# Seven-product output in one more tile, even and odd output rows, padded sums: a fused sparse attention and bilinear FFN on one Trainium2 core

## The chip, the cores and the metric

The kernel runs on one core of a Trainium2 chip. The metric is the device time in microseconds (us) of one execution. The program is one launch, with all inputs and outputs in DRAM (HBM). The page and the answers quoted below come from one profiled execution on that core.

## The reference: what is computed

The inputs are q, k and v of shape (8, 8, 576, 64) in float32 (batch, heads, sequence, head width), and three weight matrices.

```
scores = (q @ k^T) / 8
heads 0..3: keep pairs with 0 <= i - j < 32            (local)
heads 4..7: keep pairs with j <= i and i % 32 == j % 32 (strided)
attn   = softmax(scores) @ v
x      = attn as (8*576 = 4608 tokens, 8*64 = 512)
out    = ((x @ w_a) * (x @ w_b)) @ w_out
```

`w_a` and `w_b` are 512 x 1536 and `w_out` is 1536 x 512. The output is 4608 x 512 in float32.

## The kernel before

**Tiles and slots.** The FFN runs over nine tiles of 512 tokens (t = 0 to 8). Each tile is 16 slots. Slots 0 to 11 of a tile are `ffn_ab`: for one block f of 128 hidden columns, PE makes a = x w_a and b = x w_b in two PSUM banks (L545), ACT copies a to SBUF (L562), and DVE multiplies it by b into the bf16 tile `pf` (L565 or L567). Slots 12 to 15 multiply `pf` by `w_out`, a quarter of the tile's output work each. The attention of the next batch is laid between the slots by hand (`STEPS`, `LATER`): S steps are scores (PE L356), ACT's exponential (L364) and DVE's mask (L374); V steps multiply by v (PE L410 or L454), take the inverse of the sums on ACT (L463, L464), and write `xT` on DVE (L468, L470; in batches 0 and 1 it is DVE L418 and L433).

**Order.** The order of each engine's queue is the order in which the Python code issues its instructions; there is no reordering scheduler. `do(i, fn, ...)` puts a call at the end of slot i, counted over all tiles (slot 16 t + s). A wait is set by the tile framework wherever an instruction touches memory that an earlier one of another engine wrote or still reads. In many slots POOL copies one element of the slot's result (`pace`, L880), so that POOL's loads behind it are not issued too early.

**The output in two ways.** `ffn_y` (L726) is the plain product: for each 128 tokens, twelve matmuls of 128x512 (L730), one ACT copy (L736) and one store from the SP queue (L738). `ffn_ys` (L714) is used in the tiles that `FAST_Y` lists. It takes pairs of f blocks (g = 0 to 5, e = 0 or 1), halves of the tokens (i = 0 or 1) and halves of the output columns as a 2 x 2 block product, and computes it with seven products in place of eight. It needs

- sums of weights, `wf` (five kinds n, two DVE instructions each, `fast_w`, L174);
- sums and differences of `pf`, `ps` (five kinds, made by DVE in `fast_s`: L578 for kind 0, L580 for kinds 1 and 2, L582 for kinds 3 and 4), in seven instructions per tile at slots 4, 6, 8, 10, 11, 11 and 12, which cover pairs 0 to 1, 2 to 3, 2 to 5 or 4 to 5 (`slice(z0, z1)`);
- `y_plan` (L610): the products in the order 3, 4, 1, 7, 5, 2, 6, each of 2 x 6 matmuls of 128x256 (L650). The stationary operand is a slice of `pf` (products 3 and 4) or of `ps` (the rest). q = 0 or 1 chooses which 128 of a half's 256 tokens. Product 1 reads kind 0, product 5 kind 1, product 2 kind 2, product 6 kind 3, product 7 kind 4.

After the products ACT copies (L622, L633, L635), DVE adds (L626, L629, L631, L639), and POOL subtracts (issued by L824's helper, two per tile). `store_half` writes one half i in two stores from SP (`y_store`, L603 to L605), one for each q.

**The last tile.** `y_tail` (L656) makes the same products with q as the outer loop, so that the first half of the rows is stored while the second is computed. For q = 0 each product has its own bank. For q = 1 products 3, 5 and 4, 2 use the two banks of a tile `o`, and products 1, 6 and 7 the two banks of a tile `st`. The last product is cut in two, the second part in a bank of its own.

**Memory shared.** `ps` has the same buffer as the early loads of batches 0 and 1 (`shared`). `wf` is made in slots 33 to 42, that is in tile 2.

Of the kernel before, what the change touches and what calls it, by code (L numbers as in the profile page):

```python
# [7 lines left out]
F32 = mybir.dt.float32  # L8
BF16 = mybir.dt.bfloat16
I16 = mybir.dt.int16  # L10
ALU = mybir.AluOpType
# [12 lines left out]
PW = 344  # L24
VW = 128
WCH = (0, 2, 5, 8, 10, 12)
FAST_Y = (3, 4, 5, 6, 7, 8)


@with_exitstack  # L30
def kernel(
# [10 lines left out]
    nc = tc.nc  # L42
# [7 lines left out]
    FD = d_ff // 128  # L50
    TTOK = 512
# [6 lines left out]
    nat = ctx.enter_context(tc.tile_pool(name="nat", bufs=1))  # L58
    sb = ctx.enter_context(tc.tile_pool(name="sb", bufs=3))
    fsb = ctx.enter_context(tc.tile_pool(name="ffn", bufs=2))  # L60
    pst = ctx.enter_context(tc.tile_pool(name="pst", bufs=1, space=bass.MemoryType.PSUM))
    dram = ctx.enter_context(tc.tile_pool(name="dram", bufs=2, space=bass.MemoryType.DRAM))

    psum4 = {}
# [98 lines left out]

    FG = FD // 2
    HT = TTOK // 2
    HN = d_model // 2
    wf = wp.tile([128, 5, FG, HN], BF16, name="wf")
    wov = wo_sb.rearrange("p (g e) (j n) -> p e j g n", e=2, j=2)
# [14 lines left out]
    shared = {}  # L183

    def load_qk(b, strided, heads=range(HL), names="kq"):
        for nm in names:
            src = {"k": k, "q": q}[nm]
            if b < FIRST_D:
                n, R, h0 = (NP, RS, HL) if strided else (96, RL, 0)
                w0 = {"k6": 0, "q6": 1536, "k8": 3072, "q8": 5120}[f"{nm}{R}"]  # L190
                if b not in shared:
                    shared[b] = nat.tile([128, 5 * FD * TTOK // 4], BF16, tag="shared", name="shared")
                t = nats[b, nm, strided] = shared[b][:n, w0:w0 + HL * R * D].rearrange("p (h r d) -> p h r d", r=R, d=D)
                hs = slice(heads[0], heads[-1] + 1)
                nc.gpsimd.dma_start(out=t[:, hs], in_=src[b, h0:h0 + HL].rearrange("h (p r) d -> p h r d", r=R)[:, hs])  # L195
            elif strided:

                t = nat_s[nm]
                n = 32 if b == FIRST_D else YS
                for h in heads:  # L200
                    nc.gpsimd.dma_start(
                        out=t[32 * h:32 * h + n],
                        in_=bass.AP(tensor=src.tensor, offset=(b * H + HL + h) * S * D,
                                    ap=[[RS * D, n], [YS * RS * D, 3], [1, RS * D]]))
            else:
                if 0 in heads:
                    nats[b, nm, strided] = nat.tile([128, NY, D], BF16, tag=f"{nm}l", name=f"{nm}l")
                t = nats[b, nm, strided]
                for h in heads:
                    nc.gpsimd.dma_start(out=t[32 * h:32 * h + 32],  # L210
                                        in_=src[b, h].rearrange("(i y) d -> y i d", y=32))
            nats[b, nm, strided] = t
# [127 lines left out]
    ps = {}  # L340
# [190 lines left out]
    def mm_bank(shape):  # L531
        nm = "tp" if used[0] % 4 == 3 and used[0] >= 0 else "mm"
        used[0] += 1
        return psum4[nm].tile(shape, F32, tag=nm, name="mm")
# [13 lines left out]
    def ffn_ab(t, f, mid, ab=None):  # L548
# [13 lines left out]
        nc.scalar.copy(a_sb, ab[0])  # L562
        if t in FAST_Y:
            halves = lambda x: x.rearrange("p (a i s) -> p a i s", i=2, s=16)
# [5 lines left out]
    pss = {}  # L570

    def fast_s(t, n, gs):
        if t not in pss:
            pss[t] = nat.tile([128, 5 * FD * TTOK // 4], BF16, tag="shared", name="ps").rearrange("p (g m) -> p g m", g=FG)
        s = pss[t][:, gs]
        x = pfs[t].rearrange("p (g e) (i m) -> p g e i m", e=2, i=2)[:, gs]
        if n == 0:
            nc.vector.tensor_tensor(s[:, :, 0:HT], x[:, :, 0, 0], x[:, :, 1, 1], op=ALU.add)  # L578
        elif n == 1:
            nc.vector.tensor_tensor(s[:, :, HT:3 * HT].rearrange("p g (i m) -> p g i m", i=2), x[:, :, 0], x[:, :, 1], op=ALU.add)  # L580
        else:
            nc.vector.tensor_tensor(s[:, :, 3 * HT:].rearrange("p g (e m) -> p g e m", e=2), x[:, :, :, 1], x[:, :, :, 0],  # L582
                                    op=ALU.subtract)

    yst = {}

    def products(t):
        pf, s = pfs[t], pss[t]
        full = lambda e, i: (lambda g, q: pf[:, 2 * g + e, HT * i + 128 * q:HT * i + 128 * (q + 1)])
        summed = lambda n: (lambda g, q: s[:, g, HT * n + 128 * q:HT * n + 128 * (q + 1)])  # L590
        wsum = lambda n: (lambda g: wf[:, n, g])
        wfull = lambda e, j: (lambda g: wov[:, e, j, g])
        return {"3": ("a", full(0, 0), wsum(0)), "4": ("b", full(1, 1), wsum(1)), "1": ("c", summed(0), wsum(2)),
                "2": ("b", summed(2), wfull(0, 0)), "5": ("a", summed(1), wfull(1, 1)), "6": ("c", summed(3), wsum(3)),
                "7": ("d", summed(4), wsum(4))}
# [5 lines left out]
        return slice(HN * j, HN * (j + 1))  # L601

    def y_store(eng, t, y, i, q, n=slice(0, d_model)):  # L603
        rows = out[TTOK * t:TTOK * (t + 1), n].rearrange("(q a i s) c -> a s i q c", q=2, i=2, s=16)
        eng.dma_start(out=rows[:, :, i, q], in_=y[i][:, q, n])  # L605

    def y_bufs():
# [2 lines left out]
    def y_plan(t):  # L610

        plan, bank, v = products(t), {}, {}
        y = []

        def store_half(i):
            for q in range(2):
                y_store(nc.sync, t, y, i, q)

        def post(k):
            if k == "3":  # L620
                v["a"] = v["w"] = f32t("ya")
                nc.scalar.copy(v["a"], bank["a"])  # L622
                y.extend(y_bufs())
                v["y"] = y
            elif k == "4":
                nc.vector.tensor_tensor(v["w"], bank["b"], v["a"], op=ALU.add)  # L626
            elif k == "1":
                v["e"] = f32t("ye")
                nc.vector.tensor_tensor(v["e"], bank["c"], v["w"], op=ALU.add)  # L629
            elif k == "7":  # L630
                nc.vector.tensor_tensor(v["e"], v["e"], bank["d"], op=ALU.subtract)  # L631
            elif k == "2":
                nc.scalar.copy(y[1][:, :, col(0)], bank["b"])  # L633
            elif k == "5":
                nc.scalar.copy(y[0][:, :, col(1)], bank["a"])  # L635
                do(16 * t + 15, nc.gpsimd.tensor_tensor, y[0][:, :, col(0)], v["e"], y[0][:, :, col(1)], ALU.subtract)
                do(16 * t + 18, store_half, 0)
            else:
                nc.vector.tensor_tensor(v["w"], bank["c"], v["w"], op=ALU.add)  # L639
                do(16 * t + 17, nc.gpsimd.tensor_tensor, y[1][:, :, col(1)], v["w"], y[1][:, :, col(0)], ALU.subtract)  # L640
                do(16 * t + 19, store_half, 1)

        for k in "3417526":
            b, lhs, rhs = plan[k]
            new = b not in bank
            if new:
                bank[b] = mm_bank([128, 2, HN])
            for q in range(2):
                for g in range(FG):
                    nc.tensor.matmul(bank[b][:, q], lhsT=lhs(g, q), rhs=rhs(g), start=new and q == 0 and g == 0,  # L650
                                     stop=g == FG - 1, skip_group_check=True)
                    if g == FG - 1 and q == 1:
                        post(k)
                    yield v

    def y_tail(t):  # L656

        plan, y = products(t), y_bufs()
        w, e = f32t("ya"), f32t("ye")
        v = {"a": w, "y": y}  # L660
        for q in range(2):
            if q == 0:
                bank = {x: mm_bank([128, HN]) for x in "abcd"}
            else:
                o = psum4["o"].tile([128, 2, 512], F32, tag="o", name="end")
                st = pst.tile([128, 2, 512], F32, tag="st", name="end")
                bank = {"a": o[:, 0, :HN], "b": o[:, 1, :HN], "c": st[:, 0, :HN], "d": st[:, 1, :HN]}
            c21, c12, c22 = y[1][:, q, col(0)], y[0][:, q, col(1)], y[1][:, q, col(1)]
            wq, eq = w[:, q], e[:, q]
            seen = set()  # L670
            for k in "3412567":
                b, lhs, rhs = plan[k]
# [69 lines left out]
    with tc.manual_schedule(engines={ENG.PE, ENG.SP, ENG.Pool, ENG.DVE, ENG.Activation}):  # L742
# [10 lines left out]
        for x, src in ((raw[0], k), (raw[1], q)):  # L753
            nc.sync.dma_start(out=x[:96].rearrange("p (h r d) -> p h r d", h=2, d=D),
                              in_=src[0, 0:2].rearrange("h (p r) d -> p h r d", r=RL))
# [67 lines left out]
        def do(i, fn, *args):  # L823
            at.setdefault(i, []).append(lambda: fn(*args))  # L824
# [7 lines left out]
        for b in range(FIRST_D, B):  # L832
# [7 lines left out]
            else:  # L840
# [5 lines left out]
            gs = {2: (13, 13, 14, 14, 15, 16, 17, 17, 18, 18), 3: (8, 9, 10, 11, 12, 13, 14, 15, 16, 17)}.get(b) or (  # L846
                3, 5, 7, 9, 12, 13, 14, 15, 16, 17)
# [10 lines left out]
        do(17, rezero, 1)  # L858
        do(18, fill_v, vl_buf[1])
        do(19, fill_v, vs_buf[1])  # L860
        for n in range(5):
            for z in range(2):
                do(33 + 2 * n + z, fast_w, n, slice(3 * z, 3 * z + 3))
        for g in range(FG):
            for n in range(3 if g < FG - 1 else 1):
                do(16 * (NT - 1) + 2 * g + 1, fast_s, NT - 1, n, slice(g, g + 1))
# [45 lines left out]
```

The softmax here doesn't subtract the row's maximum and nothing guards it: scores larger than these inputs give would overflow.

## Time and profile before

| what | value |
|---|---|
| median of three runs | 337.68 us (337.02 to 338.57) |
| the profiled execution | 336.98 us, of which the span 335.3 us |
| mean granted TensorE clock | 0.998 |
| PE busy | 326.2 us, 97% |
| DVE busy | 254.7 us, 76% |
| ACT busy | 202.8 us, 60% |
| POOL busy | 173.4 us, 52% |
| moved by DMA | 37.60 MB, mean 112 GB/s |

The span runs from the first instruction to the last; 1.7 us of the profiled execution lie outside it. Busy shares are means over the whole span: the sections about 40 slices and the answers for single windows tell where an engine is full. A time such as 158.01 is counted from the start of the span. In a timeline line the first number is the start, the second how long the group of x instructions lasted from its first start to its last end. Matmuls overlap: a matmul of 128x512 is listed with 379 ns, but six of them follow each other in 1.30 us, so each takes 0.216 us of PE; eighty-four of 128x256 take 9.17 us, 0.109 us each. "Idle before" is the time that an engine stood still ahead of an instruction, and the releaser is who ended it.

### The profile page before, as it was taken

What the parts mean: (1) busy time and instruction counts of PE and PEld (TensorE: products, weight loads), DVE (VectorE), ACT (ScalarE), POOL (GpSimd) and SP (SyncE); (2) the same over time, 40 slices, a digit from 0 to 9 for tenths busy, and PEclk for the clock granted to TensorE, in tenths of its full rate; (3) what the DMA queues carried; (4) which work ended last, traced back from release to release, by engine and by line L of the source; (5) the groups of instructions that cost most, each with busy time, mean ns of one, the idle gap of its engine ahead of it and who ended that gap; (6) DMA issues with size and microseconds to landing.
All of it is one profiled execution on the core that took longest, in us unless ns stands there. A gap on an engine that the chain in (4) does not pass through costs nothing.

```text
span 335.3 us, 7662 instructions
## 1 busy us (share of the span) xinstructions
PE 326.2 (97%) x2814; PEld 201.8 (60%) x2814; DVE 254.7 (76%) x489; ACT 202.8 (60%) x329; POOL 173.4 (52%) x295
## 2 busy tenths in 40 slices
PE   8999999999999999999999999999999999999992
PEld 6654555455555555556999885568556844674472
DVE  5867566768878985799999999999877845738641
ACT  5663955468678865776587757875788533223320
POOL 8945836499956644765577457754312031312011
PEclk9999999999999999999999999999999999999999
DMA  9999999599999599969888998899123021003013
GB/s 155 148 203 196 201 181 188 120 191 70 131 221 155 86 99 158 129 116 92 69 83 139 179 98 75 142 164 107 25 62 119 2 73 54 1 12 116 0 29 98
DMA packets 102173, 37.60 MB, mean 112 GB/s; under 512 B 77432, under 2 KB 97784, under 8 KB 102136
## 3 DMA queue, kind: packets, MB, share of 16 engines
q0 software_dynamic: 87760, 19.58, 64.4%
q1 hardware_dynamic: 14104, 17.34, 17.7%
q8 instruction: 22, 0.36, 0.4%
q10 hardware_dynamic: 272, 0.20, 0.2%
q14 instruction: 15, 0.12, 0.1%
HBM read 39.71 MB, written 9.44 MB: 147 GB/s over the span
## 4 chain that ended last, share of the span: by engine, by line
PE 75%; DMA 12%; POOL 7%; DVE 2%; issue 2%; ACT 0%; DVEq 0%; POOLq 0%
PE mm L545 44%; PE mm L650 14%; PE mm L730 7%; DMA vl<-in_v_dram 4%; PE o L454 4%; PE st L356 3%; DMA shared<-in_k_dram 3%; DMA wa_sb<-in_moe_w_a_dram 3%; PE end L678 1%; PE mm L678 1%; POOL shared L195 1%; DMA kl<-in_k_dram 1%; POOL ql L210 1%; DMA natk<-in_k_dram 1%; POOL vl L222 1%
## 5 line engine op out<-in xcount | busy, mean ns | idle before, releaser
L545 PE MATMUL mm<-xT,wb_sb 128*128 128x512 bf16 (+1 forms) x472 | 110.2, 357 | 0.1
L545 PE MATMUL mm<-xT,wa_sb 128*128 128x512 bf16 (+1 forms) x472 | 110.3, 358 | 0.0
L562 ACT COPY a_sb<-mm 128x512 f32<-128x512 f32 x106 | 62.2, 587 | 48.7 <-PE mm L545 46.4
L545 PEld LDWEIGHTS <-wb_sb 128*128 128x128 bf16 x480 | 46.4, 98 | 44.5 <-issue 0.6
L880 POOL CAST pace<-pf 1x1 f32<-1x1 bf16 x84 | 28.4, 339 | 85.1 <-DVE pf L565 73.8
L565 DVE TENSOR_TENSOR pf<-a_sb,mm 128x512 bf16<-128x512 f32 x72 | 48.5, 674 | 17.2 <-PE mm L545 13.8
L545 PEld LDWEIGHTS <-wa_sb 128*128 128x128 bf16 x480 | 42.6, 98 | 31.2
L364 ACT ACTIVATE p<-st 128x576 bf16<-128x576 f32 (+1 forms) x64 | 41.7, 651 | 9.5 <-PE st L356 9.0
L463 ACT ACTIVATE xr<-o 64x576 f32<-64x576 f32 x48 | 31.1, 648 | 26.1 <-PE o L454 25.9
L730 PE MATMUL mm<-wo_sb,pf 128*128 128x512 bf16 x144 | 34.4, 379 | 0.5 <-DMA wo_sb<-in_moe_w_out_dram 0.5
L464 ACT ACTIVATE xr<-xr 64x576 f32<-64x576 f32 x48 | 32.9, 685 | 1.5
L650 PEld LDWEIGHTS <-ps 128*128 128x128 bf16 x300 | 28.5, 98 | 4.4 <-DVE ps L578 1.2
L567 DVE TENSOR_TENSOR pf<-a_sb,mm 128x512 bf16<-128x512 f32 x34 | 23.0, 678 | 8.4 <-ACT a_sb L562 5.9
L470 DVE TENSOR_TENSOR xT<-o,xr 64x288 bf16<-64x288 f32 x48 | 21.5, 448 | 10.4 <-ACT xr L464 9.7
L468 DVE TENSOR_TENSOR xT<-o,xr 64x288 bf16<-64x288 f32 x48 | 21.5, 447 | 8.9 <-ACT xr L464 8.3
L374 DVE TENSOR_TENSOR p<-p,mask_l 128x576 int16<-128x576 int16 x32 | 19.8, 618 | 6.8 <-ACT p L364 6.7
L650 PE MATMUL mm<-wf,ps 128*128 128x256 bf16 x180 | 22.7, 273 | 0.1
L234 POOL DMA_DIRECT2D vs<-in_v_dram x24 | 19.7, 821 | 4.1 <-PE st L356 2.8
L730 PEld LDWEIGHTS <-pf 128*128 128x128 bf16 x144 | 12.9, 98 | 13.9 <-issue 0.8
L880 POOL COPY pace<-y_sb 1x1 f32<-1x1 f32 x18 | 3.2, 177 | 34.0 <-ACT y_sb L633 14.8
L210 POOL DMA_DIRECT2D ql<-in_q_dram x24 | 16.0, 666 | 6.2 <-DMA wo_sb<-in_moe_w_out_dram 4.2
L210 POOL DMA_DIRECT2D kl<-in_k_dram x24 | 16.1, 671 | 4.0 <-issue 3.8
(155 smaller groups left out, 493.7 us busy)
## 6 DMA issues: line engine op xcount, KB each, us to landing
out_dram<-y_sb SPq DMA_DIRECT2D x34, 256.0 KB
vl<-in_v_dram POOLq DMA_DIRECT2D x7, 384.0 KB, 7.2
kl<-in_k_dram POOLq DMA_DIRECT2D x24, 72.0 KB, 3.1
ql<-in_q_dram POOLq DMA_DIRECT2D x24, 72.0 KB, 3.2
vs<-in_v_dram POOLq DMA_DIRECT2D x24, 72.0 KB, 3.8
wo_sb<-in_moe_w_out_dram POOLq DMA_DIRECT2D x4, 384.0 KB, 11.2
natk<-in_k_dram POOLq DMA_DIRECT2D x20, 72.0 KB, 3.2
natq<-in_q_dram POOLq DMA_DIRECT2D x20, 72.0 KB, 3.5
```

Of the source, the lines that this page charges most:

```text
L210: nc.gpsimd.dma_start(out=t[32 * h:32 * h + 32], in_=src[b, h].rearrange("(i y) d -> y i d", y=32))
L364: nc.scalar.activation(p[:M, :, :W], st[:M, :, :W], ACT.Exp, scale=scale)
L463: nc.scalar.activation(r, sums, ACT.Ln)
L464: nc.scalar.activation(r, r, ACT.Exp, scale=-1.0)
L468: nc.vector.tensor_mul(dst[:, W * half:W * (half + 1)], o[:64, j, :W], r[:, j])
L545: nc.tensor.matmul(ps_[:, c0:c0 + n], lhsT=w[:, kk, 128 * f:128 * (f + 1)], rhs=xT[:, kk, x0:x0 + n], start=(kk == first and c0 == 0), sto ...
L562: nc.scalar.copy(a_sb, ab[0])
L565: nc.vector.tensor_mul(pf[:, f, :].rearrange("p (i a s) -> p a i s", i=2, s=16), halves(a_sb), halves(ab[1]))
L567: nc.vector.tensor_mul(pf[:, f, :], a_sb, ab[1])
L650: nc.tensor.matmul(bank[b][:, q], lhsT=lhs(g, q), rhs=rhs(g), start=new and q == 0 and g == 0, stop=g == FG - 1, skip_group_check=True)
L730: nc.tensor.matmul(y, lhsT=pf[:, f, 128 * j:128 * (j + 1)], rhs=wo_sb[:, f], start=(f == 0), stop=(f == FD - 1))
L880: nc.gpsimd.tensor_copy(pace, done)
```

## The change

The change has five parts.

1. `FAST_Y` gets tile 2: its output is made by `ffn_ys` (84 matmuls of 128x256, with the sums on DVE) and no longer by `ffn_y` (48 of 128x512).
2. The ten `fast_w` instructions move from slots 33 to 42 to earlier ones: five at the end of slot 12 in tile 0, two at slot 16, one each at 19, 20 and 22 in tile 1.
3. q now chooses even or odd tokens of a half in place of its first or second 128. The stationary slices of `pf` and `ps` step by two elements. A row pair is adjacent in DRAM, so `store_half` becomes one store of 128 partitions x 4 KB where it was two of 128 x 2 KB. The outermost dimension of the output's access pattern is 16 where it was 8, in the last tile's stores too.
4. The five kinds of sums in `ps` are laid 272 elements apart (`SW`), not 256, so that `fast_s` writes a pattern of three levels (pairs, kinds, tokens) where it was two.
5. In `y_tail`, q = 1, each of the products' banks is a tile of its own: a in `o`, b in `st`, c and d in two of the `mm` banks.

The source lines of the changed kernel are one later from L167 on up to `fast_s` (L174 becomes L175, L578, L580, L582 become L579, L581, L583); the matmuls L650 and L678 keep their numbers.

```diff
-FAST_Y = (3, 4, 5, 6, 7, 8)
+FAST_Y = (2, 3, 4, 5, 6, 7, 8)
...
+    SW = HT + 16
...
-                    shared[b] = nat.tile([128, 5 * FD * TTOK // 4], BF16, tag="shared", name="shared")
+                    shared[b] = nat.tile([128, FG * 5 * SW], BF16, tag="shared", name="shared")
...
     def fast_s(t, n, gs):
         if t not in pss:
-            pss[t] = nat.tile([128, 5 * FD * TTOK // 4], BF16, tag="shared", name="ps").rearrange("p (g m) -> p g m", g=FG)
-        s = pss[t][:, gs]
+            pss[t] = nat.tile([128, FG * 5 * SW], BF16, tag="shared", name="ps").rearrange("p (g n m) -> p g n m", g=FG, n=5)
+        s = pss[t][:, gs, :, :HT]
         x = pfs[t].rearrange("p (g e) (i m) -> p g e i m", e=2, i=2)[:, gs]
         if n == 0:
-            nc.vector.tensor_tensor(s[:, :, 0:HT], x[:, :, 0, 0], x[:, :, 1, 1], op=ALU.add)
+            nc.vector.tensor_tensor(s[:, :, 0], x[:, :, 0, 0], x[:, :, 1, 1], op=ALU.add)
         elif n == 1:
-            nc.vector.tensor_tensor(s[:, :, HT:3 * HT].rearrange("p g (i m) -> p g i m", i=2), x[:, :, 0], x[:, :, 1], op=ALU.add)
-        else:
-            nc.vector.tensor_tensor(s[:, :, 3 * HT:].rearrange("p g (e m) -> p g e m", e=2), x[:, :, :, 1], x[:, :, :, 0],
-                                    op=ALU.subtract)
+            nc.vector.tensor_tensor(s[:, :, 1:3], x[:, :, 0], x[:, :, 1], op=ALU.add)
+        else:
+            nc.vector.tensor_tensor(s[:, :, 3:], x[:, :, :, 1], x[:, :, :, 0], op=ALU.subtract)
...
-        full = lambda e, i: (lambda g, q: pf[:, 2 * g + e, HT * i + 128 * q:HT * i + 128 * (q + 1)])
-        summed = lambda n: (lambda g, q: s[:, g, HT * n + 128 * q:HT * n + 128 * (q + 1)])
+        full = lambda e, i: (lambda g, q: pf[:, 2 * g + e, HT * i + q:HT * (i + 1):2])
+        summed = lambda n: (lambda g, q: s[:, g, n, q:HT:2])
...
     def y_store(eng, t, y, i, q, n=slice(0, d_model)):
-        rows = out[TTOK * t:TTOK * (t + 1), n].rearrange("(q a i s) c -> a s i q c", q=2, i=2, s=16)
+        rows = out[TTOK * t:TTOK * (t + 1), n].rearrange("(a i s q) c -> a s i q c", i=2, s=8, q=2)
...
         def store_half(i):
-            for q in range(2):
-                y_store(nc.sync, t, y, i, q)
+            rows = out[TTOK * t:TTOK * (t + 1)].rearrange("(a i s q) c -> a s i (q c)", i=2, s=8, q=2)
+            nc.sync.dma_start(out=rows[:, :, i], in_=y[i].rearrange("p q c -> p (q c)"))
...
             else:
-                o = psum4["o"].tile([128, 2, 512], F32, tag="o", name="end")
-                st = pst.tile([128, 2, 512], F32, tag="st", name="end")
-                bank = {"a": o[:, 0, :HN], "b": o[:, 1, :HN], "c": st[:, 0, :HN], "d": st[:, 1, :HN]}
+                bank = {"a": psum4["o"].tile([128, 2, 512], F32, tag="o", name="end")[:, 0, :HN],
+                        "b": pst.tile([128, 2, 512], F32, tag="st", name="end")[:, 0, :HN],
+                        "c": mm_bank([128, HN]), "d": mm_bank([128, HN])}
...
-        for n in range(5):
-            for z in range(2):
-                do(33 + 2 * n + z, fast_w, n, slice(3 * z, 3 * z + 3))
+        for n, slot in enumerate((16, 16, 19, 20, 22)):
+            do(12, fast_w, n, slice(0, 3))
+            do(slot, fast_w, n, slice(3, 6))
```

## The prediction

> **What bounds the kernel now.** I read the page's busy shares first, then the 40 slices, the chain, the waits, and the timelines of the stages that the change touches.
>
> ```profile
> PE 326.2 (97%) x2814; PEld 201.8 (60%) x2814; DVE 254.7 (76%) x489; ACT 202.8 (60%) x329; POOL 173.4 (52%) x295
> PE   8999999999999999999999999999999999999992
> DVE  5867566768878985799999999999877845738641
> ...
> PE mm L545 44%; PE mm L650 14%; PE mm L730 7%; DMA vl<-in_v_dram 4%; PE o L454 4%; PE st L356 3%; DMA shared<-in_k_dram 3%; DMA wa_sb<-in_moe_w_a_dram 3%; PE end L678 1%; PE mm L678 1%; POOL shared L195 1%; DMA kl<-in_k_dram 1%; POOL ql L210 1%; DMA natk<-in_k_dram 1%; POOL vl L222 1%
> ```
>
> PE is full from slice 2 to the last but one, so a microsecond taken from PE or added to it is a microsecond of the end. DVE stands at nine tenths from tile 3 on: it hides little more there. The waits show that PE waits for DVE in the output stage already, at product 1 ("times" 4, one a tile):
>
> ```profile
> PEld L650 <- DVE ps L578: 1.2, 4, 0.3
> ```
>
> The two timelines of tile 3's output stage decide this forecast (start, us, engine, line; x is the count). DVE:
>
> ```profile
> 156.73 0.91 DVE L470 TENSOR_TENSOR xT<-o,xr 64x288 bf16<-64x288 f32 x2
> 157.67 0.69 DVE L578 TENSOR_TENSOR ps<-pf 128x1024 bf16<-128x1024 bf16 x1
> 158.28 0.68 DVE L582 TENSOR_TENSOR ps<-pf 128x1024 bf16<-128x1024 bf16 x1
> 158.88 0.45 DVE L374 TENSOR_TENSOR p<-p,mask_s 72x576 int16<-72x576 int16 x1
> 159.25 0.70 DVE L304 STREAM_TRANSPOSE tk<-natk 128x512 bf16<-128x512 bf16 x1
> 159.88 1.18 DVE L580 TENSOR_TENSOR ps<-pf 128x2048 bf16<-128x2048 bf16 x1
> ```
>
> PE, same stretch:
>
> ```profile
> 155.13 2.46 PE L650 MATMUL mm<-wf,pf 128*128 128x256 bf16 x21
> ...
> 158.01 1.24 PE L650 MATMUL mm<-wf,ps 128*128 128x256 bf16 x8
> 159.09 0.42 PE L454 MATMUL o<-p,vs 72*128 72x72 bf16 x8
> ```
>
> Product 1 starts at 158.01, just behind L578, its own sum. The last sum, L580 for pairs 2 to 5 (kinds 1 and 2), ends at 161.06, 3 us later. Before, nobody needs it until product 5.
>
> The tail (tile 8, q = 1) has three stops of PE:
>
> ```profile
> 324.78 0.82 PE L678 MATMUL end<-wf,pf 128*128 128x256 bf16 x6 [0.46 <-ACT ya L683]
> 327.46 0.81 PE L678 MATMUL end<-wo_sb,ps 128*128 128x256 bf16 x6 [0.46 <-ACT y_sb L693]
> 329.51 0.49 PE L678 MATMUL end<-wf,ps 128*128 128x128 bf16 x6 [0.58 <-DVE y_sb L703]
> ```
>
> Two products share a two-bank tile, so each waits for the reading of the other's bank.
>
> [...] No load in this trace is strided. Contiguous ones take 98 ns, and in the attention a load and a 72-column matmul follow each other every 32 ns, so a load that doubled would still lie under a product's 109 ns. [...] Here the clock is 0.998. [...] The stores' outer dimension is 8, [...] from 331 to 333, with stores alone, the DMA share is 0.47. [...] I keep the durations.
>
> **Part 1, tile 2's output.** Removed: 48 matmuls at 0.216 us = 10.36. Added: 84 at 0.109 = 9.17. That is -1.19 on PE, all on the path; tile 3's wait of 0.27 for L578 will come with it: -0.92. Bounds -1.2 and -0.6. DVE in tile 2 loses ten L174 (5.3 us) and gets seven sums (5.0 us, by tile 3's rows) and four adds of 0.67 (2.7 us) in a window with 6.52 busy of 11.30: covered. ACT loses one copy of 0.59. POOL gets two L824 of 1.3 us, in tile 3; tile 4 carries the same two with PE full, so nothing. SP issues four stores less in tile 2 and two more in tile 3 behind the transposed loads; those loads have several us until their use.
>
> **Part 2, weights' sums earlier.** Five L174 (0.53 each alone; in a row 0.45 to 0.5, as other unwaited ones follow: about 2.4 us) stand on DVE after the mask of step S1 (51.54 to 52.0) and ahead of V0's L418 and L433 (51.91 to 52.68). There is one `o` bank, so V1 on PE (54.34) waits for that L433: now until about 55.1. V2 waits for V1's L433 behind a mask and two L299 (1.43): about 57.65, where 56.69 stood. X1 (59.91) waits for V3's L433 likewise. I take +0.95 us on PE; bounds +0.2 (DVE idles 3.5 us before 51.54, but the in-order queue can't use it) and +1.4. The other five fall where two banks per slot leave a slot of slack, so nothing; cover: PE's next use of the same bank, 1 us later.
>
> **Parts 3 and 4, the waits.** I followed the built program's waits to the instruction that raises each count. Before, product 1's weight load for g = 2 waits for L578 (pairs 2 to 5), and the next load that waits for a sum belongs to product 7. After, g = 2 waits for the same sum, and **g = 3 waits for L581's instruction for pairs 2 to 5**, the last sum of the tile. It shares no element with it: the load reads from element 4080 of `ps`, between two pieces of a write with three levels ([1360,4], [272,2], [1,256] from 2992). With two levels (before) no such wait was set. It is there in tiles 2 to 7, not in the tail, where each sum covers one pair.
>
> Its price, by tile: end of L580 less the time at which g = 3 starts (product 1's start + 3 x 0.109), plus 0.04 for the signal.
>
> - Tile 3: 161.06 + 0.04 - (158.01 + 0.33) = 2.76 us.
> - Tiles 4 and 5: L580 ends at 195.53 and 229.76, g = 3 at 192.81 and 227.04: 2.76 each.
> - Tile 6 (263.39 and 261.27): 2.16. Tile 7 (292.36 and 291.89): 0.51.
> - Tile 2 has tile 3's order: 2.76.
>
> Sum **+13.7 us**. Can DVE come earlier? Its sums stand behind L470 of V5, which waits for ACT and so for a matmul just ahead of the output stage; L578, L582, mask, transpose and L580 then follow without a gap. None of them needs what PE holds back, so the gap neither closes nor becomes a deadlock. Queued behind the waiting load are V6, the rest of the products, and by them ACT's and DVE's later work: all shift together. Lower bound 2 us in tiles 2 to 5 if DVE, with less left over from the tile ahead, comes earlier (in sum +10.5); upper 3.3 (in sum +16). [...]
>
> Strided loads: 0; bounds 0 and 588 matmuls x 4 ns = 2.5. Larger, fewer stores in the middle: 0, for no one waits for them.
>
> **Part 5, the tail.** Without the three stops PE runs 3 to 7 at 0.655 per product: product 7 begins at 327.45, not 329.51. Then POOL ends the chain: L693 at 326.7, two L694/L699 of 0.73 to 328.3, two L706 to 328.9, where 330.67 stood: -1.74. The last store is issued until 329.6 and not 331.3; [...] the rest drains in 1.3 and not 1.8 us. Sum -2.1; bounds -1.4 [...] and -2.6.
>
> **The sum.** -0.95 + 0.95 + 13.7 - 2.1 = +11.6 us. On the profiled execution's 336.98 that is 348.6; the median lies 0.7 above that execution (337.68), so I say 348.9.
>
> **Rivals.** (a) *The new wait ends before PE comes to it*, and the tail decides. For it: PE's waits before name L578 alone. Against: L580's end at 161.06. It decides if that end comes within 3.2 us of the stage's start, where it now takes 5.9. Then 337.68 - 2.1 = 335.6: faster. (b) *Strided loads [...] set the pace.* For it: no strided load is in the trace. [...] At 120 ns, 588 x 11 ns = 6.5 us more: 355. (c) *DVE drops [...] on the padded write*: L580 at 2.2 us, 6 x 1 us more, and gaps near 3.8 us that may cost clock: 356. (d) *Half of the gap is taken back*, since a PE that waits lets DVE catch up: +5 to +8: 344.
>
> **Chances.** Main 0.76, (a) 0.10, (b) and (c) 0.07, (d) 0.07. The bounds of the main case give about 345 to 352; with (d) 343.5 to 352.5 leaves out (a) and (b, c). A measurement of this kernel tells about 0.5% (1.7 us) from no change: faster 0.09, same 0.03, slower 0.88.
>
> **What would show it.** Right: the waits list PE L650 behind DVE ps L581, about 13 us over six tiles; the stage from V5 to the next tile's L545 takes 13.2 us in tiles 3 to 5, not 10.4; the tail has no stop of 0.46; the stores run at twice the DMA share. Part 2 right: PE's V1 and V2 in tile 0 wait for L433. Wrong: no L581 in PE's waits, products' matmuls over 0.11 us apart, or L581 much longer than 1.2 us.

## The result, and the profile after

| | before | after |
|---|---|---|
| median | 337.27 us (335.94 to 338.57, 6 runs) | 351.74 us (349.22 to 357.62, 6 runs) |
| profiled execution, span | 336.98 us, 335.3 us | 349.22 us, 347.2 us |
| mean granted TensorE clock | 0.998 | 0.989 |

The ratio of the times is 1.0401, with a 95% interval of 1.0351 to 1.0452: the change makes the kernel slower. Two of after's six runs, 354.82 and 357.62 us, count as slow, and the ratio is that of the fast runs alone. The two profiled executions lie 12.2 us apart, their spans 11.9.

The page of after, with its busy shares, three rows of the 40 slices and the chain by line:

```profile
PE 328.0 (94%) x2850; PEld 206.9 (60%) x2850; DVE 264.3 (76%) x500; ACT 201.9 (58%) x328; POOL 175.5 (51%) x296
...
PE   8999998999999979997999799997999799999995
...
DVE  6866659778678978998899959997778644656752
...
PEclk9999999999999999999999989999999899999999
...
PE mm L546 47%; PE mm L650 12%; DMA shared<-in_q_dram 4%; PE o L455 4%; PE mm L730 4%; DMA wo_sb<-in_moe_w_out_dram 3%; PE st L357 3%; DMA ql<-in_q_dram 2%; DVE ps L581 2%; DMA vl<-in_v_dram 2%; PE mm L678 2%; POOL shared L196 1%; DVE xT L471 1%; DVE ps L579 1%; ACT xr L464 1%
```

PE's busy time has grown by 1.8 us only, and the span by 11.9: PE stands still. The row of slices has a dent in each of tiles 2 to 6, and DVE's line L581 is on the chain at 2%, where before has no line of the sums. The waits of PE's weight loads (us in total, times, longest):

```profile
PEld L650 <- DVE ps L581: 13.0, 6, 2.6
PEld L411 <- DVE xr L434: 2.7, 3, 1.2
PEld L650 <- DVE ps L579: 1.5, 5, 0.3
```

The first line is new: six waits, one in each of tiles 2 to 7, for the last sum. Here is tile 3's output stage, DVE first:

```profile
158.46 0.91 DVE L471 TENSOR_TENSOR xT<-o,xr 64x288 bf16<-64x288 f32 x2
159.41 0.69 DVE L579 TENSOR_TENSOR ps<-pf 128x1024 bf16<-128x1024 bf16 x1
160.01 0.69 DVE L583 TENSOR_TENSOR ps<-pf 128x1024 bf16<-128x1024 bf16 x1
160.62 0.45 DVE L375 TENSOR_TENSOR p<-p,mask_s 72x576 int16<-72x576 int16 x1
160.99 0.70 DVE L305 STREAM_TRANSPOSE tk<-natk 128x512 bf16<-128x512 bf16 x1
161.61 1.18 DVE L581 TENSOR_TENSOR ps<-pf 128x2048 bf16<-128x2048 bf16 x1
```

PE, same stretch (the bracket is the idle time ahead, and who ended it):

```profile
159.75 0.69 PE L650 MATMUL mm<-wf,ps 128*128 128x256 bf16 x3
162.85 0.72 PE L650 MATMUL mm<-wf,ps 128*128 128x256 bf16 x5 [2.41 <-DVE ps L581]
163.41 0.42 PE L455 MATMUL o<-p,vs 72*128 72x72 bf16 x8
163.67 1.91 PE L650 MATMUL mm<-wf,ps 128*128 128x256 bf16 x16
```

Product 1 makes three of its matmuls, stands still until L581 ends at 162.79, and goes on with g = 3. Before, all eight followed each other but for 0.3 us, in which the load for g = 2 waited for L578, its own sum; that short wait is in after too. DVE's six instructions are the same, in the same order, with the same durations.

The tail's second half has no stop any more (it had three):

```profile
338.55 1.47 PE L678 MATMUL end<-wf,pf 128*128 128x256 bf16 x12
339.86 0.82 PE L678 MATMUL mm<-wf,ps 128*128 128x256 bf16 x6
340.61 1.47 PE L678 MATMUL end<-wo_sb,ps 128*128 128x256 bf16 x12
341.92 1.49 PE L678 MATMUL mm<-wf,ps 128*128 128x256 bf16 x18
```

The best ledger is the length of each tile on PE, from its first matmul of L545 (L546) to that of the next tile; from tile 2 to tile 7 these are steady to 0.01 us between kernels where nothing differs. The columns e1 to e9 are the experiments below.

| us | before | after | e1 | e3 | e4 | e5 | e9 |
|---|---|---|---|---|---|---|---|
| tile 2 | 35.21 | 36.82 | 34.23 | 35.21 | 35.64 | 35.21 | 41.92 |
| tile 3 | 34.23 | 36.81 | 34.23 | 38.48 | 35.64 | 34.23 | 41.45 |
| tile 4 | 34.47 | 38.41 | 34.48 | 38.53 | 35.88 | 34.47 | 41.33 |
| tile 5 | 34.22 | 36.82 | 34.23 | 36.81 | 35.64 | 34.23 | 41.03 |
| tile 6 | 33.98 | 37.62 | 33.97 | 37.61 | 35.38 | 33.97 | 40.44 |
| tile 7 | 29.89 | 30.44 | 29.89 | 30.44 | 30.21 | 29.89 | 34.28 |
| tile 8 to the end | 37.18 | 34.07 | 34.41 | 35.56 | 34.05 | 35.92 | 34.08 |

After less before: 1.61 + 2.58 + 3.94 + 2.60 + 3.64 + 0.55 - 3.11 = 11.81; tile 2 begins 0.13 later; together 11.9, the whole difference.

Tiles 4 and 6 are longer than the wait makes them. The cause is seen when tile 4's output stage is cut at the edges of the clock's steps. The columns are the stretch, its length, busy time of PE, PEld, DVE, ACT and POOL (counts in brackets), **the granted clock**, DMA share and GB/s:

```profile
192.52:195.94 3.42, 3.42 (x39) 3.08 (x38) 3.25 (x6) 2.58 (x5) 1.81 (x3) 1.00 0.90 83
195.94:199.35 3.41, 1.53 (x19) 0.99 (x16) 3.37 (x7) 0.80 (x2) 2.68 (x4) 1.00 0.96 111
199.35:202.76 3.41, 2.85 (x20) 2.17 (x21) 1.10 (x2) 1.06 (x2) 0.00 (x0) 0.50 0.88 75
202.76:206.18 3.42, 3.42 (x39) 3.09 (x38) 2.78 (x5) 1.08 (x3) 0.12 (x1) 1.00 0.03 5
```

For 3.41 us the clock is half. PE stood still for 2.41 us, of which 1.88 fell into the stretch ahead. Tile 6 shows the same from 274.45 to 277.86, after a stop of 1.82 us; tiles 2, 3 and 5, with the same 2.41, don't. The six runs of after are ordered alike by time and by mean clock, from 349.22 us at 0.989 to 357.62 at 0.966. More such stretches in the longer runs would give this; only the first run was profiled, so it is not shown.

### The profile page after: what moved, and what is told of

It reads as the page before. It is cut to its first block, busy times and chain, and to the rows that moved or that the text cites. A ratio compares the mean times of both kernels' runs of the same rounds, so it can differ in the third digit from the quotient of the medians.

```text
span 347.2 us, 7724 instructions
## 1 busy us (share of the span) xinstructions
PE 328.0 (94%) x2850; PEld 206.9 (60%) x2850; DVE 264.3 (76%) x500; ACT 201.9 (58%) x328; POOL 175.5 (51%) x296
## 4 chain that ended last, share of the span: by engine, by line
PE 72%; DMA 11%; DVE 8%; ACT 3%; POOL 3%; issue 2%; DVEq 0%; POOLq 0%
PE mm L546 47%; PE mm L650 12%; DMA shared<-in_q_dram 4%; PE o L455 4%; PE mm L730 4%; DMA wo_sb<-in_moe_w_out_dram 3%; PE st L357 3%; DMA ql<-in_q_dram 2%; DVE ps L581 2%; DMA vl<-in_v_dram 2%; PE mm L678 2%; POOL shared L196 1%; DVE xT L471 1%; DVE ps L579 1%; ACT xr L464 1%
## 5 line engine op out<-in xcount | busy, mean ns | idle before, releaser
L546 PE MATMUL mm<-xT,wb_sb 128*128 128x512 bf16 (+1 forms) x472 | 110.2, 357 | 0.1
L546 PE MATMUL mm<-xT,wa_sb 128*128 128x512 bf16 (+1 forms) x472 | 110.3, 358 | 0.0
L546 PEld LDWEIGHTS <-wb_sb 128*128 128x128 bf16 x480 | 46.4, 98 | 44.4 <-issue 0.6
L546 PEld LDWEIGHTS <-wa_sb 128*128 128x128 bf16 x480 | 42.6, 98 | 31.2
L650 PEld LDWEIGHTS <-ps 128*128 128x128 bf16 x360 | 35.3, 101 | 19.3 <-DVE ps L581 13.0
L650 PE MATMUL mm<-wf,ps 128*128 128x256 bf16 x216 | 30.9, 290 | 12.0 <-DVE ps L581 11.8
L375 DVE TENSOR_TENSOR p<-p,mask_l 128x576 int16<-128x576 int16 x32 | 22.3, 698 | 3.6 <-ACT p L365 3.6
L730 PE MATMUL mm<-wo_sb,pf 128*128 128x512 bf16 x96 | 23.2, 379 | 0.0
L650 PE MATMUL mm<-wf,pf 128*128 128x256 bf16 x144 | 17.5, 273 | 0.0
```

What stands on the lines that cost most here:

```text
L375: nc.vector.tensor_tensor(pi, pi, mk, op=ALU.bitwise_and)
L546: nc.tensor.matmul(ps_[:, c0:c0 + n], lhsT=w[:, kk, 128 * f:128 * (f + 1)], rhs=xT[:, kk, x0:x0 + n], start=(kk == first and c0 == 0), sto ...
L730: nc.tensor.matmul(y, lhsT=pf[:, f, 128 * j:128 * (j + 1)], rhs=wo_sb[:, f], start=(f == 0), stop=(f == FD - 1))
```

## The experiments

Theory W: the loss is product 1's wait for the last sum. Which part of the change sets it was the first question, since the change has two candidates in the same tiles, the step-2 loads (part 3) and the padded sums (part 4).

### e1: the sums kind by kind

```diff
-            pss[t] = nat.tile([128, FG * 5 * SW], BF16, tag="shared", name="ps").rearrange("p (g n m) -> p g n m", g=FG, n=5)
+            pss[t] = nat.tile([128, FG * 5 * SW], BF16, tag="shared", name="ps").rearrange("p (n g m) -> p g n m", g=FG, n=5)
```

> After, with one edit: the sums of a tile lie kind by kind (all pairs of kind 0, then all pairs of kind 1, ...) instead of pair by pair. Padding, step-2 loads, one-bank tail, merged stores, seven products in tile 2 and the early weights' sums all stay. Theory W (the loss is the wait of product 1's fourth weight load for the last sum, set because a step-2 read and a write that runs around it are taken as overlapping): the write of kinds 1 and 2 no longer runs around kind 0, so the wait goes, and with it 13 us of PE idle and the two stretches at half clock: the time is 351.7 - 13.5 - 2.7 = 335.5 us (334.5 to 336.5), PE's waits name no L581 over 0.3 us in sum, and no slice shows a clock under 0.95 after slice 2. Rival C (the step-2 loads, the padding or the stores cost time by themselves): nothing of that changed, the time stays at 349 to 352 us. Rival H (half the loss is this wait, half something else): 342 to 345 us.

Measured: 335.50 us, against 337.19 for before in the same comparison, ratio 0.9952 (0.9931 to 0.9973). In the output stages of tiles 2 to 7, PE and its loads have one line left on the sums:

```profile
PEld L650 <- DVE ps L579: 1.5, 5, 0.3
```

L581 still ends at 162.28 in tile 3, as late against the stage as in after, and product 1 no longer asks for it: it starts at 159.22 and makes its eight matmuls in one go.

```profile
159.22 1.24 PE L650 MATMUL mm<-wf,ps 128*128 128x256 bf16 x8
```

The clock row has no step below 9 in any of its 40 slices. Tiles 3 to 7 are as long as before to 0.01 us. So one line in which the layout is chosen takes away the whole loss, half clock included, while the step-2 loads, the padding, the larger stores and the padded writes are all still there: in the middle of the kernel these cost nothing. Rivals C and H are out.

The tail, though, has a wait that after doesn't have:

```profile
PEld L678 <- DVE ps L581: 0.5, 1, 0.5
322.44 1.49 PE L678 MATMUL mm<-wo_sb,ps 128*128 128x256 bf16 x12 [0.26 <-DVE ps L581]
```

In the tail each sum covers one pair. Product 2 reads kind 2 from pair 0 on, and now its first load waits for the sum of kinds 1 and 2 of pair 5: kind by kind, the two pieces of that write have kind 2 of pairs 0 to 4 between them. PE's and DVE's work in the tail ends 31.04 us after the start of tile 8, where after has 30.69. The new layout moved the wait to a place where it is short; it is not free of it.

### e2: padding alone

```diff
-            pss[t] = nat.tile([128, 5 * FD * TTOK // 4], BF16, tag="shared", name="ps").rearrange("p (g m) -> p g m", g=FG)
+            pss[t] = nat.tile([128, FG * 5 * SW], BF16, tag="shared", name="ps").rearrange("p (g n m) -> p g n m", g=FG, n=5)
...
```

on the kernel before, with `fast_s` as in after and the loads contiguous.

> Before, with the padded sums alone (rows of 272 elements for 256, each sum written with a pattern of three levels); loads contiguous, rows of the output as before, five products' weights as before. The reason in the prediction (theory P: the three-level write makes the wait): the wait of L581 appears in tiles 3 to 7, 3 x 2.76 + 2.16 + 0.51 = 10.95 us: 348 us. Theory W (the step-2 read makes it): no wait, no change: 337.3 us, within 0.5%. Rival D (DVE slower on a padded write): L581 near 2.3 us instead of 1.18, time 340 us or more.

Measured: 337.49 us, ratio 1.0004 (0.9984 to 1.0024). PE's loads wait for L579 as before (line numbers are after's here), and no line names L581:

```profile
PEld L650 <- DVE ps L579: 1.2, 4, 0.3
```

L581 takes 1.18 us, with three levels as with two. Theory P falls: the padded write alone makes no wait.

### e3: even and odd rows alone

```diff
-        full = lambda e, i: (lambda g, q: pf[:, 2 * g + e, HT * i + 128 * q:HT * i + 128 * (q + 1)])
-        summed = lambda n: (lambda g, q: s[:, g, HT * n + 128 * q:HT * n + 128 * (q + 1)])
+        full = lambda e, i: (lambda g, q: pf[:, 2 * g + e, HT * i + q:HT * (i + 1):2])
+        summed = lambda n: (lambda g, q: s[:, g, HT * n + q:HT * (n + 1):2])
...
```

on the kernel before, with after's stores and the sums unpadded.

> Before, with even and odd output rows alone (step-2 weight loads of pf and ps, one store for each half of a tile), sums not padded, the write of the last sum with two levels. Theory W: the wait for L580 appears in tiles 3 to 7: 3 x 2.76 + 2.16 + 0.51 = 10.95 us, less 0.5 to 1.3 for the shorter drain, plus 0 to 3 where the clock falls to half after a gap: 347 to 350 us. Theory P (the padded three-level write makes the wait): no such wait, 336 to 337 us. Rival C (step-2 loads slow PE): products' matmuls further apart than 0.109 us.

Measured: 352.93 us, ratio 1.0476 (1.0428 to 1.0525); the profiled execution 351.70.

```profile
PEld L650 <- DVE ps L580: 10.4, 5, 2.6
```

The wait is there in tiles 3 to 7, with the step-2 read and a write of two levels. The time lies 3 us above the expected range. The ledger says why: tiles 3, 4 and 6 have the half clock (at 162.92, 200.47 and 275.56, 1.5 to 1.7 us each, where the range allowed for 3 in all), and tile 1 is 37.5 us long where before has 35.9, in which a transfer for DVE's L304 came late and held PE through L470 for 1.7 us. Such a wait of 0.9 to 1.7 us in tile 1 is in most profiles of the experiments, of kernels with and without the early weights' sums. Products' matmuls stay 0.109 us apart where the clock is whole.

e1, e2 and e3 together: the wait needs a read with a step of two **and** a write that runs around what is read. In the layout pair by pair the last sum writes kinds 1 and 2 of pairs 2 to 5, and kind 0 of pair 3 lies between two of its pieces. Kind by kind, nothing of kind 0 lies inside it. Pair 2's kind 0, which g = 2 reads, lies ahead of the write's first piece, and g = 2 doesn't wait for it; in e1's tail the wait is at the read that came to lie inside. That the framework compares patterns in this way is read from these cases; its own test was not looked at.

### e4 and e9: the wait made shorter and longer

```diff
-            for slot, n, z0, z1 in ((4, 0, 0, 2), (6, 2, 0, 2), (8, 1, 0, 2), (10, 2, 2, 4), (11, 0, 2, 6), (11, 2, 4, 6),
-                                    (12, 1, 2, 6)):
+            for slot, n, z0, z1 in ((4, 0, 0, 2), (6, 2, 0, 2), (8, 1, 0, 2), (10, 2, 2, 4), (11, 0, 2, 6), (11, 1, 2, 6),
+                                    (11, 2, 4, 6)):
```

> After, with the same instructions in another order: the last sum (kinds 1 and 2, pairs 2 to 5) stands directly behind the sum of kind 0 for pairs 2 to 5, ahead of the sum of kinds 3 and 4. A dose of the same wait: L581 then ends 1.18 us behind L579's end, so product 1's fourth load waits about 1.1 us and not 2.76 in tiles 2 to 5, about 1.1 in tile 6. Theory W: 351.7 - 4 x 1.65 - 1.0 = 344.1 us; if the half clock comes only after gaps near 2 us or longer, another 2.7 less: 341.4. So 340.5 to 344.5, with L650's waits for L581 at about 6 us in sum instead of 13. Rival C (time lost elsewhere than in this wait): 349 to 352. If the half clock comes with any gap, windows at 0.50 remain.

Measured: 342.12 us (340.69 to 342.52), ratio to before 1.0134 (1.0101 to 1.0166), with the clock whole (0.998). In tile 3:

```profile
162.14 0.39 PE L650 MATMUL mm<-wf,ps 128*128 128x256 bf16 x2 [0.85 <-DVE ps L581]
162.74 0.50 PE L650 MATMUL mm<-wf,ps 128*128 128x256 bf16 x3 [0.21 <-DVE ps L583]
```

By the ratios to before (1.0401 for after, 1.0134 here, 0.9952 in e1) the order of two instructions takes back about 9 us of 15, and with stops of 0.85 us the clock stayed at 0.998. Tiles 2 to 6 are 1.41 us longer than in e1, not 2.58.

e9 is the other direction:

```diff
-            for slot, n, z0, z1 in ((4, 0, 0, 2), (6, 2, 0, 2), (8, 1, 0, 2), (10, 2, 2, 4), (11, 0, 2, 6), (11, 2, 4, 6),
+            for slot, n, z0, z1 in ((4, 0, 0, 2), (6, 2, 0, 2), (8, 1, 0, 2), (10, 2, 2, 4), (11, 0, 2, 6), (11, 2, 4, 6), (11, 2, 4, 6), (11, 2, 4, 6), (11, 2, 4, 6),
```

> After, with the sum of kinds 3 and 4 for pairs 4 and 5 made four times over instead of once, so that the last sum stands 3 x 0.65 = 1.95 us later on DVE (the result is the same). A dose of the wait in the other direction: PE's idle before product 1's fourth load grows from 2.41 to about 4.35 us in tiles 2 to 5 and from 1.8 to about 3.8 in tile 6. Theory W: 351.7 + 5 x 1.95 = 361.5 us before any change of the clock. Theory G for the half clock (PE's activity is weighed in fixed stretches of 3.41 us, and a stretch with more than about 2 us of idle time is followed by one at half clock): with 4.35 us of idle time one of the stretches always holds over 2 us, so all of tiles 2 to 5 show a stretch at 0.50, and tile 6 too, at 1.4 to 1.7 us each instead of in two or three tiles: 364 to 367 us, with the half stretches starting whole multiples of 3.41 us apart. Rival N (the half clock comes by chance, whatever the gap): two or three stretches at 0.50, 361 to 362 us. Rival A (DVE's extra sums fall into idle time): 352 to 355.

Measured: 373.56 us (373.08 to 374.66). The stop is 4.59 us in tiles 2 to 5 and 3.99 in tile 6. All tiles from 2 to 6 show the half clock, as theory G wanted (tile 7 too, with a stop of 2.54), but tiles 2 to 6 for two stretches each and not for one, which puts the time 6.6 us above the expected range. Tile 2, in stretches cut at the clock's steps:

```profile
125.95:129.36 3.41, 0.00 (x0) 0.00 (x0) 3.34 (x6) 0.00 (x0) 1.43 (x2) 1.00 1.22 119
129.36:132.78 3.42, 2.66 (x19) 2.00 (x20) 1.31 (x2) 0.86 (x2) 0.00 (x0) 0.50 0.13 17
132.78:136.19 3.41, 3.41 (x18) 2.35 (x17) 2.78 (x5) 0.47 (x1) 0.00 (x0) 0.50 0.00 0
136.19:139.60 3.41, 3.41 (x39) 3.07 (x38) 0.42 (x1) 2.35 (x4) 1.39 (x3) 1.00 0.01 2
```

The first line is a stretch in which PE does nothing; the clock halves in the next. In that one PE is busy 2.66 of 3.41 us, and the clock stays half for another. The last section puts these stages side by side.

### e5: the tail's banks alone

Part 5 of the change (one-bank tiles for a, b, c and d), on the kernel before.

> Before, with the one-bank tiles in the tail's second half alone; rows and stores as before [...]. Theory T (the three stops of PE in the tail are waits for the other bank of a shared tile, and the drain is shortened by the stores' shape and not by the banks): PE's part, -1.7 to -1.9 us, drain after DVE's last instruction as before (4.6 us): 337.2 - 1.8 = 335.4 us (335.0 to 335.8). Rival S (the drain gets shorter by the earlier end alone): -3.1 us, 334.1. Rival P (POOL's subtractions set the end anyway): 337.2.

Measured: 336.10 us against 337.83, ratio 0.9941 (0.9920 to 0.9962), -1.7 us by the medians; the time is 0.3 us above the expected range. In the profile the last L706 ends 30.69 us after tile 8's start (before 32.56, after 30.69): PE's and DVE's part is -1.87, as expected. But the drain, the time from that end, DVE's last, to the end of the span, is 5.24 us and not as before: before has 4.62, and after 3.38. Single microseconds of the drain, e5 and then after (stores alone; the figure before the last is the DMA share):

```profile
329.20:330.20 1.00, 0.00 (x0) 0.00 (x0) 0.00 (x0) 0.00 (x0) 0.00 (x0) 1.00 0.46 132
330.20:331.20 1.00, 0.00 (x0) 0.00 (x0) 0.00 (x0) 0.00 (x0) 0.00 (x0) 1.00 0.53 173
```

```profile
344.20:345.20 1.00, 0.00 (x0) 0.00 (x0) 0.00 (x0) 0.00 (x0) 0.00 (x0) 1.00 0.81 233
```

With rows as before the share is 0.46 and 0.53, and the drain is longer where PE is faster (5.24 us for 4.62); with even and odd rows the share is 0.81. With even and odd rows and before's banks (e3) the drain is 3.00 us. In the ledger the rows alone (e3) take 1.62 us off the tail, the banks alone (e5) 1.26, both (after) 3.11. That both together are worth more than their sum isn't shown: the four profiles with before's tail (before, e2, e6, e7) have 37.00 to 37.30 us there.

### e6 and e7: the weights' sums early, and tile 2

e6 is before with the ten `fast_w` calls as in after; e7 is that with tile 2 in `FAST_Y`.

> Before, with the ten weights' sums made in tiles 0 and 1 alone (five of them in one row on DVE in tile 0's output stage); tile 2 keeps the plain output. Theory Q (V1 and V2 of tile 0 wait for the copy out of the one o bank that stands behind the row of five): +0.95 us: 338.1 (337.6 to 338.6), with PE waiting 0.7 and 0.2 us for DVE's L433 where before has 0.2 in all. Rival I (DVE's idle time ahead of the mask swallows it): 337.2. Rival R (DVE's relief in tile 2 gives it back): below 337.

> Before, with the early weights' sums and the seven-product output in tile 2; rows, sums and tail as before. Theory Q: the two cancel, -0.92 + 0.95: 337.2 us (336.7 to 337.8); against the kernel with the early sums alone 0.9 less. Rival V (tile 2 meets a new wait on DVE): 338 or more. Rival G (seven products save more than their matmuls): 336 or less.

Measured: e6 338.06 us, ratio 1.0014 (0.9992 to 1.0035), that is between -0.3 and +1.2 us, which doesn't settle a cost of 0.95; e7 337.46, ratio 0.9994 (0.9972 to 1.0016). The traces say it. In e6, tile 0:

```profile
59.12 0.36 PE L410 MATMUL o<-vl,p 128*128 128x65 bf16 x6 [0.73 <-DVE xr L433]
61.51 0.36 PE L410 MATMUL o<-vl,p 128*128 128x65 bf16 x6 [0.21 <-DVE xr L433]
```

V1 and V2 wait for L433, 0.94 us in all where before has 0.19 (this execution had the half clock from 15 to 25 us, so the stage begins some 4 us later than in the others; the waits compare). In e7 tile 2 is 34.22 us long, 0.99 less than before.

### e8 and e10: towards a better kernel

e8 is e1 with the five weights' sums of tile 0 ahead of step S1, in DVE's idle time:

```diff
-            do(12, fast_w, n, slice(0, 3))
...
+            if i == 12:
+                for n in range(5):
+                    fast_w(n, slice(0, 3))
             take(i)
```

> The kernel with the sums kind by kind (335.5 us), with the five weights' sums of tile 0 put ahead of step S1's mask, where DVE idles 2.8 us, instead of behind it. Theory Q: the two waits of V1 and V2 go, -0.9 us: 334.6 us (334.0 to 335.0). Rival L (the sums then wait for the late fourth part of wo_sb, and the mask behind them): 335.5 or more.

Measured: 334.24 us (333.95 to 335.18), ratio 0.9904 (0.9866 to 0.9942). DVE in tile 0:

```profile
48.15 2.42 DVE L175 TENSOR_TENSOR wf<-wo_sb 128x768 bf16<-128x768 bf16 x5
52.08 0.46 DVE L375 TENSOR_TENSOR p<-p,mask_l 128x576 int16<-128x576 int16 x1 [1.51 <-ACT p L365]
```

The row of five ends before the mask's input comes, and PE has no wait at V1, and 0.19 at V2 as before. e8 is faster than both kernels, than before by 1.0%. Its tail has e1's wait too, 0.27 us of PE.

> The kernel with sums kind by kind and the five weights' sums ahead of S1's mask (334.2 us), with the first transpose of the third batch's natk moved one slot later in tile 1 (two transposes in slot 25 of the plan, none in 24). In several profiles DVE waits there up to 3 us for the natk transfer, and L471, which stands behind it on DVE, then holds PE by 0.9 to 1.7 us. Theory D (that wait is real in most runs): 333.4 us (333.0 to 333.9), tile 1 35.9 us long instead of 37.0. Rival E (the transfer is late anyway, the wait moves to the next L471 behind the two transposes): 334.2 or more.

Measured: 334.41 us (three runs at 333.14 to 333.63, three at 335.19 to 335.23), ratio 0.9891 (0.9847 to 0.9936). In its profile tile 1 is 36.3 us long, not 37.0, but the median doesn't move and lies 0.5 us above the expected range: inconclusive. What sets its two groups of times was not found.

## Why the prediction was right

348.9 us was predicted with 343.5 to 352.5, and 351.74 was measured: the direction, the place and the size of the wait were right. The reason given for it was wrong, the wait's price left a term out, and three other terms were off, in part against each other.

- **Parts 3 and 4, the wait.** Predicted 2.76 us in each of tiles 2 to 5, 2.16 and 0.51 in tiles 6 and 7. The lengths of tiles 3, 5 and 7, which kept their clock, grew by 2.58, 2.60 and 0.55; the trace lists PE idle for 2.41 ahead of g = 3. The 0.18 too much has a reason. The price counts g = 3 from product 1's start at 158.01, "just behind L578". But L578 starts at 157.67 and ends at 158.36, and g = 2 waits for it, the 0.3 us that the prediction lists itself:

```profile
158.42 0.55 PEld L650 LDWEIGHTS <-ps 128*128 128x128 bf16 x6 [0.31 <-DVE ps L578]
```

  So g = 3 began near 158.53 in before and not at 158.34. From the sum's end to the load it took 0.06 us in after's tile 3 (162.79 to 162.85) and in before's (158.36 to 158.42), where the price has 0.04. Tile 7 isn't among the four tiles with this wait, and there the price isn't too high. Rivals (a) and (d) fell: neither did the wait end early, nor did DVE catch up.
- **The reason for the wait.** The prediction laid it to the write with three levels, and said that with two no such wait was set. e2 has that write and no wait; e3 has two levels and the wait. It takes the step-2 read, against a write whose pieces lie on both sides of it. Only the fact that the wait was in the program carried the forecast, not its explanation.
- **The clock: no term.** That the wait would leave the granted clock whole was the author's estimate, shown by no trace, and it failed. Gaps of 2.41 and 1.82 us were followed by 3.41 us of half clock in tiles 4 and 6: tile 4 grew by 3.94, 1.36 more than tiles 3 and 5. Tile 6 grew by 3.64; with the 0.18 that the wait came short elsewhere taken off its 2.16, some 1.7 is the clock's. Together about 3 us that the sum didn't have. The mean clock of the other runs is at or below that of the profiled one, which fits as many such stretches or more; the median lies 2.8 us above 348.9.
- **Strided loads, padded writes, merged stores: 0.** Right, as e1's tiles show. The mean of a step-2 load from `pf` in after is 98 ns, as for the contiguous ones in before; in e3 the products' matmuls stay 0.109 us apart, and the sum of 2048 elements (L580, L581) has a mean of 1.19 us in before and, padded, in after. The prediction's 0, its 4 ns a load and the 120 ns and 2.2 us of (b) and (c) were the author's estimates. Rivals (b) and (c) fell.
- **Part 1.** -0.92 predicted; -0.99 in e7.
- **Part 2.** +0.95 predicted; the waits came as told (0.73 and 0.21 us in after too), but tile 2 starts only 0.13 late. In the profiled execution of before, PE had waited in the same stage for a weight transfer, which the prediction took as given:

```profile
48.22 0.81 PE L730 MATMUL mm<-wo_sb,pf 128*128 128x512 bf16 x3 [0.47 <-DMA wo_sb<-in_moe_w_out_dram]
```

  In after this wait is missing. Tile 0 without such a wait is 37.24 us long in after, e6 and e7, which have the early sums, and 36.32 in e5, which hasn't: 0.92, close to the term. Waits for transfers in the first 100 us differ between the runs (0.47 us here and none in after, 1.7 in e3's tile 1), and a term of 1 us there is within what two executions differ by.
- **Part 5, the tail.** -2.1 predicted; -3.11 measured. PE's part was -1.74 and became -1.87; the drain's was -0.5 and became -1.24. The prediction shortened only the last 1.8 us, to 1.3, by the author's estimate. Each of before's last three microseconds with traffic (330.30 to 333.30) has a share of 0.37 to 0.48, which fits a backlog of earlier stores that shrinks too; a backlog was not shown. The share of 0.81 in after (from 344.20) is 1.7 times the 0.47 that the prediction read in before (331 to 333), not twice. e3 shows the shorter drain without a faster PE: 3.00 for 4.62.

On the spans of the profiled executions the forecast is 11.6 and the result 11.9 us because these cancel: +3.0 (clock) - 1.0 (tail) - 0.8 (part 2's cover) - 0.9 (five waits of 0.18). That the sum came so close is luck.

Four sums of the prediction don't come out. Its last step adds 0.7 to 348.6, which is 349.3 and not 348.9. The terms' bounds add up to 344.6 and 353.1, and to 355.6 with the 2.5 for the loads, not to "345 to 352". Part 1 is -0.92 in its paragraph and -0.95 in the sum, and part 5's -1.74 and -0.5 make -2.2 and not -2.1; these two change little.

## What to carry to other kernels

In this framework a wait can be set between patterns that share no element: when a read gets a step, look at every write that still has pieces on both sides of it, and lay the buffer so that what one consumer reads is one block. Then look again at the places where the writes come in another order, as in e1's tail. Where such a wait can't be avoided, put the producer that it names first; here two swapped instructions were worth about 9 us. Price a stop of PE by its idle time and by the clock behind it (2.41 us idle and then 3.41 us at half clock in after's tile 4). A compute tail faster by 1.87 us took 1.26 off the stretch from tile 8 to the end with the stores as before (e5), and 3.11 with the merged ones (after).

## What the runs showed of the hardware

**The steps of the granted clock lay on a grid of 3.413 us.** The steps to half clock within one execution lie whole multiples of 3.413 us apart: 199.35 and 274.45 in after (22 stretches), and 129.37, 170.33, 211.29, 252.25, 293.21 and 330.76 in e9 (12 each, the last 11). With the trace cut at that grid, PE's busy time in a stretch and the clock of the next go together in these stages:

| kernel | stage | PE busy in the stretch, us | its clock | clock of the next |
|---|---|---|---|---|
| e9 | tiles 2 to 7 | 0.00, 0.50, 1.23, 1.36, 1.43, 0.87 | 1.00 | 0.50 |
| e3 | tiles 3, 4, 6 | 1.00, 1.31, 1.57 | 1.00 | 0.50 |
| after | tiles 4, 6 | 1.53, 1.57 | 1.00 | 0.50 |
| after | tiles 2, 3, 5 (lowest) | 1.63, 2.02, 2.15 | 1.00 | 1.00 |
| e3 | tile 5 (lowest) | 2.05 | 1.00 | 1.00 |
| e9 | tiles 2, 3, 4, 5, 6 | 2.66, 1.70, 0.98, 0.85, 1.38 | 0.50 | 0.50 |
| after, e3 | tile 4 | 2.86, 3.08 | 0.50 | 1.00 |

In these stages the step from whole to half clock comes after a stretch with PE busy 1.57 us or less of 3.41 and not at 1.63; from half clock PE returns after a stretch with 2.86 or more, and not with 2.66. So a stop of 2.41 us was followed by half clock where 1.88 us of it fell into one stretch (after's tile 4), and not in tiles 2, 3 and 5, where an edge of the grid cut it so that PE was busy 1.63 us or more on each side. Two places don't follow these figures, the end of e5 and the start of e6:

```profile
327.11:330.52 3.41, 1.46 (x20) 1.21 (x17) 0.91 (x3) 0.37 (x1) 1.37 (x2) 1.00 0.51 172
330.52:333.93 3.41, 0.00 (x0) 0.00 (x0) 0.00 (x0) 0.00 (x0) 0.00 (x0) 1.00 0.23 70
```

```profile
11.52:14.94 3.42, 2.21 (x41) 1.59 (x40) 1.94 (x5) 1.62 (x3) 3.21 (x6) 1.00 1.35 149
14.94:18.35 3.41, 3.41 (x56) 2.29 (x53) 2.36 (x6) 1.34 (x3) 2.10 (x3) 0.50 1.32 181
18.35:21.76 3.41, 3.41 (x62) 2.81 (x61) 1.53 (x5) 2.05 (x4) 0.67 (x1) 0.50 1.31 203
```

In e5 a stretch with 1.46 us busy is followed by a whole one. In e6 one with 2.21 is followed by half clock, which stays for three stretches (to 25 us) though PE is busy throughout. So PE's busy time in a profile does not account for every step, and what else plays a part was not shown. The table was drawn up from the runs that it describes; a stage made to sit at 1.6 us was not tried.

**The drain with the output's outer dimension at 16 instead of 8.** The DMA share is 0.81 in after (from 344.20 to 345.20) and 0.46 to 0.53 in e5 (329.20 to 331.20), and the time from DVE's last instruction to the end is 3.38 us instead of 5.24 with the same compute (30.69 us of tile 8 in both); with before's banks it is 3.00 (e3) instead of 4.62. How the shape does this was not shown; the engines of a single store were not counted.
